# Linear attention into an MLP: the attention's small products of a batch gathered into one place of the schedule

## The chip, the core and the metric

The kernel runs on one core of a Trainium2 chip. The core has a matrix engine (TensorE, PE in the profile; PEld is its weight load), a vector engine (VectorE, DVE), a scalar engine for activations (ScalarE, ACT), a general engine (GpSimd, POOL) and a queue engine (SyncE, SP) that here only issues DMAs. Each runs its own instructions in order and waits on semaphores for the others. Matmuls write PSUM, which the kernel uses as eight banks of 512 float32 per partition. The metric is the device time of one execution in microseconds (us), less is better.

## The reference

`q`, `k` and `v` have 8 batches, 8 heads, 576 tokens and 64 values per head. The MLP takes the attention's output as 4608 tokens of 512 values.

```python
phi = lambda x: np.where(x > 0, x, np.exp(x) - 1.0) + 1.0
q_p, k_p = phi(q), phi(k)
kv  = einsum('bhsd,bhse->bhde', k_p, v)      # 64 x 64 for each head
z   = sum(k_p, axis=2)
num = einsum('bhsd,bhde->bhse', q_p, kv)
den = einsum('bhsd,bhd->bhs', q_p, z) + 1e-06
x   = (num / den) as [4608, 512]
h   = x @ w_in                               # 512 -> 2048
g   = gelu_tanh(h)
out = g @ w_out                              # 2048 -> 512
```

## The kernel before, in words

**Tiles.** Of each batch's 576 tokens the first 512 are four chunks of 128; the last 64 are its rest tokens. The rest tokens of all eight batches are 512 as well, as four tiles m = 0 to 3, each with two batches' rests. So the MLP runs in nine groups of 512 tokens, `iteration(j)` (L739): j = 0 to 7 are the batches, j = 8 is the rests. Matmul operands are bf16, sums float32.

**A group.** It has 32 slots. Slots 0 to 15 are the h steps: four matmuls of 128x512 into one PSUM bank (`h_mm`, L380) and a gelu on ACT (L390). Slots 16 to 31 are the o steps: four output tiles, each of four slots of four matmuls (`o_mm`, L723). An o tile is copied out of PSUM when its sixteen matmuls are done (`evac`, L684: DVE for t = 0 and 2, ACT for t = 1 and 3) and stored by a DMA from ACT's queue. Groups 0 and 1 interleave their steps a little differently.

**The schedule is written out by hand.** `at(j, slot, fn)` (L498) puts a piece of work behind a slot of a group; `run` calls it there, so its instructions stand at that place in each engine's order. Nothing is reordered later.

**Attention.** phi is taken as min(max(x + 1, 1), exp(x)): `linear_of` (DVE, L226), `exp_of` (ACT, L218; the exponential and the gelu use different tables, so a table load stands before and after) and `least_of` (DVE, L232). `kv` is 72 matmuls of 64x64 weights by 65 columns (the 65th column, of ones, gives z; `kv_paired`, L248). `n` holds num and den: for batches 4 to 7 `n_quads` (L278) takes for a chunk 16 matmuls of 64x64 weights by 65 columns, four at a time in the four quarters of the array, into two banks of 4 x 65 columns. `divide` (L289) makes x of it: a reciprocal of the dens (L294) and a multiply (L295) for each bank, or one of each over a pair of banks. A DMA transpose from SP's queue brings a chunk's x into `xt`, which the next group's h steps read; others bring q's phi into `qt` and a rest tile's into `qtr`.

**PSUM.** Six banks are a pool (`ps_b`) that h, o, and some n and kv tiles share; two more are one tile, the pair (`ps_a`).

**What stands where, for batch b = 4 to 7.** It is prepared two groups before its own, in group b - 2: the maps of k and q at slots 13 to 17 or 19, v's cast at 15 (20 for b = 4). In group b - 1, slot 4 (`early`): n of chunks 1 and 0 and of rest tile m = b - 4, in one run of 48 small matmuls. Slot 22 (`late`): n of chunks 3 and 2 (32), then the 72 of kv of batch b + 1, the divides, kv's copy into bf16 (L669), and the min and the transposes of q for batch b + 1 and of the next rest tile. kv of batch 4 has a place of its own in group 3, slot 2 (L617). Batches 0 to 3 go another way (`nab`, L264) that the change leaves alone.

**Loads.** SP issues all of them in order with the transposes. Seven load buffers (`pld`) are shared by q, k, v and weights. k of batch 5 is loaded at slot 11 of group 2, its q and v at slot 23; batch 6 and 7 at slot 6 of group b - 3, behind a rest tile.

Of the kernel before, what the change touches and what calls it, by code (L numbers as in the profile page):

```python
# [9 lines left out]
BF16 = mybir.dt.bfloat16  # L10
# [5 lines left out]
def kernel(  # L16
# [12 lines left out]

    nc = tc.nc

    B, H, S, D = q.shape
    d_model, d_ff = moe_w_in.shape
    P = 128
# [15 lines left out]
    pe = ctx.enter_context(tc.tile_pool(name="pe", bufs=1))  # L52
    pphi = ctx.enter_context(tc.tile_pool(name="pphi", bufs=2))
    pt = ctx.enter_context(tc.tile_pool(name="pt", bufs=2))
    px = ctx.enter_context(tc.tile_pool(name="px", bufs=5))
    pg = ctx.enter_context(tc.tile_pool(name="pg", bufs=1))
    pout = ctx.enter_context(tc.tile_pool(name="pout", bufs=2))
    psm = ctx.enter_context(tc.tile_pool(name="psm", bufs=2))
    pkv = ctx.enter_context(tc.tile_pool(name="pkv", bufs=1))
    ps_b = ctx.enter_context(  # L60
# [15 lines left out]
    def bank(name, shape, dt=FP32):  # L76
        return ps_b.tile(shape, dt, name=name, tag="b")

    def pair_of_banks(name):
        return ps_a.tile([P, 2, 512], FP32, name=name, tag="a")  # L80
# [131 lines left out]
    def exp_of(name, b, hs=None):  # L212
        x = ld[name, b]
        hs = hs or slice(0, x.shape[1])
        if (name, b) not in exps:
            exps[name, b] = pe.tile([P, x.shape[2] // D, x.shape[1], D], BF16, name=name + "_e")
        o, i = maps_view(name, b, x, exps[name, b], hs)
        nc.scalar.activation(o, i, AF.Exp)  # L218

# [8 lines left out]
    def least_of(name, b, hs=None):  # L228
        p, e = phi[name, b], exps[name, b]
        if hs:  # L230
            p, e = p[:, :, hs, :], e[:, :, hs, :]
        nc.vector.tensor_tensor(p, p, e, op=ALU.min)  # L232
# [9 lines left out]
    def kv_paired(b, ii, kv_of):  # L242
        kp, vp = phi["k", b], vp_paired(b)
        for j in range(J):
            for s in range(2):
                for a in range(2):
                    r, u = slice(HP * a, HP * (a + 1)), 2 * ii + s
                    nc.tensor.matmul(  # L248
                        kv_of(a, ii)[HP * s : HP * (s + 1)],
                        lhsT=kp[r, j, u, :],  # L250
                        rhs=vp[r, j, u, :],
                        start=(j == 0),
                        stop=(j == J - 1),
                        skip_group_check=True,
                    )
# [15 lines left out]
    def kv_of_head(b, s, i):  # L271

        r = slice(HP * s, HP * (s + 1))
        return kvs[b % 4][r, i, :] if b > 3 else kvbds[b][r, i, E * s : E * (s + 1)]

    def n_quads(qt_c, bs, ns):

        for i in range(NP):  # L278
            for t in range(2):
                for s in range(2):  # L280
                    c = slice(HP * t, HP * (t + 1))
                    nc.tensor.matmul(  # L282
                        ns[s][c, E * i : E * (i + 1)],
                        lhsT=qt_c[HP * s : HP * (s + 1), i, c],
                        rhs=kv_of_head(bs[t], s, i),
                        skip_group_check=True,
                    )

    def divide(x_v, n_v):  # L289

        heads = tuple(slice(None) for _ in n_v.shape[:-1])
        shape = list(n_v.shape[:-1])
        r = psm.tile(shape, FP32, name="r" + "".join(str(d) for d in shape[1:]))
        nc.vector.reciprocal(r, n_v[heads + (D,)])  # L294
        nc.vector.tensor_tensor(  # L295
            x_v,
            n_v[heads + (slice(0, D),)],
            r[heads + (None,)].to_broadcast(shape + [D]),
            op=ALU.mult,
        )  # L300

    def x_tile():
        return px.tile([P, d_model], BF16, name="x")
# [1 line left out]
    def by_parity(x):  # L305
        return x.rearrange("p (u a d) -> p a u d", a=2, d=D)

    def by_half(x):
        return x.rearrange("p (i s a d) -> p s a i d", s=2, a=2, d=D)

    def nab(qt_c, b):
        x, n_ps = x_tile(), pair_of_banks("n_ps")
        nab_mm(qt_c, kvbds[b], [n_ps[:, a] for a in range(2)])
# [7 lines left out]
            divide(by_parity(x)[:, a], ns[a].rearrange("p (u e) -> p u e", e=E))  # L321
        return x

    def nab_quads(qt_c, bs):

        n_ps = pair_of_banks("n_ps")
        n_quads(qt_c, bs, [n_ps[:, s] for s in range(2)])

        def x_of():
            x = x_tile()  # L330
            n_v = n_ps[:, :, 0 : NP * E].rearrange("p s (a i e) -> p s a i e", a=2, e=E)
            divide(by_half(x), n_v)
            return x

        return x_of

    def nab_quads_in_banks(qt_c, bs):
        ns = [bank("n_ps", [P, NP * E]) for _ in range(2)]
        n_quads(qt_c, bs, ns)

        def x_of():
            x = x_tile()
            for s in range(2):
                divide(by_half(x)[:, s], ns[s].rearrange("p (a i e) -> p a i e", a=2, e=E))
            return x

        return x_of

# [149 lines left out]
    def at(j, slot, fn, *args):  # L498


        fill.setdefault((j, slot), []).append((fn, args))
# [71 lines left out]
    def plan_prepare(b, s_linear, s_exp):  # L573
        def casts():
            cast_v_paired(b, slice(0, NP), nc.vector.tensor_copy)

        order = "qk" if b < 5 else "kq"

        def exps_all():
            for n in order:  # L580
                exp_of(n, b)

        j, s = s_linear
        for i, n in enumerate(order):
            at(j, s + i, linear_of, n, b)
        at(j, s + (7 if b == 4 else 2), casts)
        j, s = s_exp
        at(j, s, exps_all)
        if b < 5:
            at(j, s + 2, least_q, b)  # L590
            at(j, s + 4, least_of, "k", b)
        else:
            at(j, s + 2, least_of, "k", b)

    def transposed_q(b, cs):
        for c in cs:
            nc.sync.dma_start_transpose(
                out=qts[b][:, c],
                in_=phi["q", b][:, c].rearrange("p h d -> p (h d)"),
            )  # L600

    def least_q(b, m=None):

        least_of("q", b)
        qts[b] = pt.tile([P, C, NP, P], BF16, name="qt")
        transposed_q(b, (0, 1))
        if m is not None:
            least_rest(m)
        transposed_q(b, (2, 3))

    def kv_in_pair(b):
        kv_ps = pair_of_banks("kv_ps")
# [28 lines left out]
    def plan_attention(b):  # L641


        j, m = b - 1, b - 4

        def pair_of_chunks(c):
            in_banks = nab_quads_in_banks(qts[b][:, c + 1], (b, b))
            in_pair = nab_quads(qts[b][:, c], (b, b))
            return (c + 1, in_banks), (c, in_pair)

        def early():
            chunks = pair_of_chunks(0)
            rest = nab_quads_in_banks(rest_qt[m], (2 * m, 2 * m + 1))
            transposed_x(b, 1, chunks[0][1]())
            x = rest()
            nc.sync.dma_start_transpose(out=xt_rest[:, :, P * m : P * (m + 1)], in_=x)
            transposed_x(b, 0, chunks[1][1]())

        def late():
            chunks = pair_of_chunks(2)  # L660
            if b + 1 < B:
                kv_ps = [bank("kv_ps", [P, 2, E]) for _ in range(2)]
                for ii in range(2):
                    kv_paired(b + 1, ii, lambda a, ii: kv_ps[a][:, ii, :])
            for c, x_of in chunks:
                transposed_x(b, c, x_of())
            if b + 1 < B:
                for a in range(2):
                    nc.vector.tensor_copy(out=kvs[(b + 1) % 4][:, 2 * a : 2 * a + 2, :], in_=kv_ps[a])  # L669
                least_q(b + 1, b - 3)  # L670

        at(j, 4, early)
        at(j, 22, late)

    def least_rest(m):
        linear_of("qr", m)
        least_of("qr", m)
        rest_qt[m] = psm.tile([P, NP, P], BF16, name="qtr")
        nc.sync.dma_start_transpose(
            out=rest_qt[m], in_=phi["qr", m][:, 0].rearrange("p h d -> p (h d)")  # L680
        )

    def evac(dst, src, on_scalar):
        (nc.scalar.copy if on_scalar else nc.vector.tensor_copy)(dst, src)  # L684
# [94 lines left out]
    at(1, 10, load_all_pairs, "k", k, 4)  # L779
    plan_prepare(3, (1, 24), (1, 23))  # L780
    at(1, 23, gelu_table)
    at(1, 29, load_rest, 0)
    at(1, 29, load_q, 4)
    at(1, 29, load_all_pairs, "v", v, 4)
    at(2, 11, load_all_pairs, "k", k, 5)
    at(2, 23, load_rest, 1)
    at(2, 23, load_q, 5)
    at(2, 23, load_all_pairs, "v", v, 5)
    at(3, 2, kv_in_pair, 4)
    for b in range(4, B):  # L790
        plan_prepare(b, (b - 2, 13), (b - 2, 15))
        plan_attention(b)
        at(b - 2, 15, exp_of, "qr", b - 4)
    at(2, 22, least_rest, 0)
    for b in range(6, B):
        at(b - 3, 6, load_rest, b - 4)
        at(b - 3, 6, load_batch, b)
    for b in range(4, B):
        at(b - 2, 15, gelu_table)

    for j in range(B + 1):
        iteration(j)
# [30 lines left out]
```

## Time and profile before

| | |
|---|---|
| median of 5 runs | 284.72 us (284.67 to 284.79) |
| the profiled execution: time, span in the trace | 284.78 us, 283.0 us |
| PE busy | 274.5 us, 97% of the span |
| ACT busy | 162.0 us, 57% |
| DVE busy | 105.9 us, 37% |
| POOL busy | 15.5 us, 5%, none after 45 us |
| h matmuls L380 (incl. the rest group) | 128.3 us |
| o matmuls L723 | 126.2 us |

The span is what the trace covers; 1.78 us of the execution's time lie around it. "Busy" of PE is the union of matmul intervals whose ends are modelled, so the view to trust for small changes is the chain of waits in order of time: it names, piece by piece, what the end of the kernel waited for.

### The profile page before, as it was taken

The numbers are of one execution on the slowest core, as the hardware profiler recorded it, in microseconds if no ns is written. First come the engines' busy times: TensorE is split into PE (matmuls) and PEld (weight loads), VectorE is DVE, ScalarE is ACT, GpSimd is POOL, SyncE is SP. The second block draws the span as 40 slices with busy tenths as digits, with TensorE's granted clock in tenths as the row PEclk, the third lists the DMA queues.
The fourth block names the chain that finished last, engine by engine and source line by source line (L and its number), as shares of the span: only waits on it lengthen the run. The fifth ranks groups of instructions, "written<-read, shape, count | busy, mean of one in ns | idle before, by whom it ended". The sixth has DMA issues, their size and how long they took to land.

```text
span 283.0 us, 5373 instructions
## 1 busy us (share of the span) xinstructions
PE 274.5 (97%) x2260; PEld 135.3 (48%) x2293; DVE 105.9 (37%) x193; ACT 162.0 (57%) x222; POOL 15.5 (5%) x22
## 2 busy tenths in 40 slices
PE   8799999999999999999999999999999999999995
PEld 3474455445454445445444544454444444444444
DVE  3850386344956342727090808081403000000001
ACT  4678878786966925693468536862650265026400
POOL 4147210000000000000000000000000000000000
PEclk9999999999999999999999999999999999999999
DMA  7999999968699867997739863025301300110022
GB/s 252 400 406 397 410 402 404 404 236 224 74 232 340 231 167 220 288 367 254 157 74 331 282 170 61 0 72 160 88 19 28 126 33 0 71 80 0 0 76 74
DMA packets 59591, 53.83 MB, mean 190 GB/s; under 512 B 35760, under 2 KB 45360, under 8 KB 59568
## 3 DMA queue, kind: packets, MB, share of 16 engines
q1 hardware_dynamic: 56784, 44.58, 52.1%
q10 hardware_dynamic: 2784, 8.91, 8.4%
q8 instruction: 18, 0.29, 0.4%
q14 instruction: 5, 0.04, 0.0%
HBM read 36.70 MB, written 9.44 MB: 163 GB/s over the span
## 4 chain that ended last, share of the span: by engine, by line
PE 93%; DMA 3%; issue 1%; SPq 1%; DVE 1%; ACT 0%
PE h_ps L380 44%; PE o_ps L723 44%; DMA v_x<-in_v_dram 3%; PE kv_ps L248 2%; PE n_ps L282 1%; PE n_ps L264 1%; PE t_ps L372 1%; SPq L92 1%; SPq L97 0%; PE t_ps L526 0%; DVE vp L237 0%; DVE x L362 0%; DVE kvbd L260 0%; DVE o_sb L684 0%; PE n_ps L353 0%
## 5 line engine op out<-in xcount | busy, mean ns | idle before, releaser
L723 PE MATMUL o_ps<-w_out_sb,g 128*128 128x512 bf16 (+2 forms) x590 | 126.2, 368 | 1.4 <-issue 0.6
L380 PE MATMUL h_ps<-xt,w_in_sb 128*128 128x512 bf16 (+1 forms) x551 | 114.4, 359 | 0.8 <-issue 0.2
L390 ACT ACTIVATE g<-h_ps 128x512 bf16<-128x512 f32 x144 | 84.9, 599 | 41.3 <-PE h_ps L380 39.6
L723 PEld LDWEIGHTS <-g 128*128 128x128 bf16 x608 | 57.5, 98 | 63.9
L380 PEld LDWEIGHTS <-w_in_sb 128*128 128x128 bf16 x628 | 57.9, 98 | 62.8
L684 ACT COPY o_sb<-o_ps 128x512 f32<-128x512 f32 (+1 forms) x19 | 10.8, 575 | 64.0 <-PE o_ps L723 62.4
L684 DVE COPY o_sb<-o_ps 128x512 f32<-128x512 f32 (+1 forms) x19 | 12.2, 647 | 72.4 <-PE o_ps L723 72.4
L295 DVE TENSOR_TENSOR x<-n_ps,r 128x256 bf16<-128x256 f32 (+1 forms) x49 | 26.4, 539 | 1.7
L294 DVE RECIPROCAL r<-n_ps 128x4 f32<-128x4 f32 (+1 forms) x49 | 9.2, 187 | 36.3 <-PE n_ps L282 26.6
L232 DVE TENSOR_TENSOR k_p<-k_p,k_e 128x2304 bf16<-128x2304 bf16 (+1 forms) x9 | 11.0, 1224 | 21.1 <-ACT k_e L218 21.0
L218 ACT ACTIVATE k_e<-k_x 128x2304 bf16<-128x2304 f32 (+1 forms) x9 | 17.1, 1904 | 1.0 <-DMA k_x<-in_k_dram 1.0
L218 ACT ACTIVATE q_e<-q_x 128x2048 bf16<-128x2048 f32 (+1 forms) x9 | 15.4, 1715 | 2.8 <-DMA q_x<-in_q_dram 2.7
L226 DVE TENSOR_SCALAR q_p<-q_x 128x2048 bf16<-128x2048 f32 (+1 forms) x9 | 9.9, 1103 | 13.4 <-DMA q_x<-in_q_dram 13.4
L232 DVE TENSOR_TENSOR q_p<-q_p,q_e 128x2048 bf16<-128x2048 bf16 (+1 forms) x9 | 9.9, 1102 | 11.4 <-ACT q_e L218 11.3
L380 PE MATMUL h_ps<-xt_rest,w_in_sb 128*128 128x512 bf16 x63 | 13.9, 380 | 0.1
L226 DVE TENSOR_SCALAR k_p<-k_x 128x2304 bf16<-128x2304 f32 (+1 forms) x9 | 11.0, 1219 | 4.2 <-DMA k_x<-in_k_dram 4.2
L237 DVE CAST vp<-v_x 128x2304 bf16<-128x2304 f32 (+1 forms) x9 | 11.0, 1226 | 1.9 <-DMA v_x<-in_v_dram 1.8
L403 ACT ACT_TABLE_LOAD x8 | 10.3, 1283 | 0.1
L412 PE MATMUL w_ps<-warm 128*128 128x512 bf16 x31 | 9.0, 449 | 1.2 <-DVE warm L181 1.2
L218 ACT ACT_TABLE_LOAD x7 | 9.0, 1283 | 0.1
L141 POOL CAST w_in_sb<-w_st 128x512 bf16<-128x512 f32 (+2 forms) x6 | 7.6, 1268 | 14.2 <-DMA w_st<-in_moe_w_in_dram 14.2
L248 PE MATMUL kv_ps<-vp,k_p 64*64 64x65 bf16 x576 | 6.6, 195 | 0.9 <-DVE vp L237 0.9
(46 smaller groups left out, 74.5 us busy)
## 6 DMA issues: line engine op xcount, KB each, us to landing
out_dram<-o_sb ACTq DMA_DIRECT2D x16, 512.0 KB, 3.1
k_x<-in_k_dram SPq DMA_DIRECT2D x7, 1152.0 KB, 9.3
v_x<-in_v_dram SPq DMA_DIRECT2D x7, 1152.0 KB, 11.8
q_x<-in_q_dram SPq DMA_DIRECT2D x6, 1024.0 KB, 7.9
w_st<-in_moe_w_in_dram SPq DMA_DIRECT2D x3, 1024.0 KB, 13.4
q_x<-in_q_dram SPq DMA_DIRECT2D x4, 512.0 KB, 8.5
w_st<-in_moe_w_out_dram SPq DMA_DIRECT2D x2, 1024.0 KB, 12.6
w_st<-in_moe_w_out_dram SPq DMA_DIRECT2D x4, 512.0 KB, 11.2
```

What stands on the lines that cost most here:

```text
L218: nc.scalar.activation(o, i, AF.Exp)
L226: nc.vector.tensor_scalar(o, i, 1.0, 1.0, op0=ALU.add, op1=ALU.max)
L232: nc.vector.tensor_tensor(p, p, e, op=ALU.min)
L237: fn(out=vp_paired(b)[:, :, us, 0:D].rearrange("p j u d -> p u j d"), in_=ld["v", b][:, us].rearrange("p u (j d) -> p u j d", d=D),)
L248: nc.tensor.matmul(kv_of(a, ii)[HP * s : HP * (s + 1)], lhsT=kp[r, j, u, :], rhs=vp[r, j, u, :], start=(j == 0), stop=(j == J - 1), skip_g ...
L294: nc.vector.reciprocal(r, n_v[heads + (D,)])
L295: nc.vector.tensor_tensor(x_v, n_v[heads + (slice(0, D),)], r[heads + (None,)].to_broadcast(shape + [D]), op=ALU.mult,)
L380: nc.tensor.matmul(h_ps[:, ts], lhsT=w_in_sb[:, c, P * m : P * (m + 1)], rhs=xt[:, c, ts], start=(c == 0), stop=(c == KM - 1), skip_group_ ...
L390: nc.scalar.activation(g[:, m, :], h_ps, AF.Gelu_apprx_tanh)
L403: nc.scalar.preload_act_table_set("gelu_apprx_tanh_and_others")
L684: (nc.scalar.copy if on_scalar else nc.vector.tensor_copy)(dst, src)
L723: nc.tensor.matmul(o_ps, lhsT=g[:, m, P * t : P * (t + 1)], rhs=w_out_sb[:, m, fs], start=(m == 0), stop=(m == MM - 1),)
```

## The change

For batches 4 to 7 `early` and `late` become one place, slot 17 of group b - 1. There the n of all four chunks is taken in one run of 64 small matmuls. Their 65-column blocks fill banks six at a time: two pool banks, two more pool banks, then the pair with the last four blocks. kv of batch b + 1 follows at once, into free columns of the pair. x becomes one tile of four chunks (`xs`, one buffer); the five divides follow each other, and each chunk's transpose is issued as soon as its part is there.

The four rest tiles are no longer spread over groups 3 to 6: their loads stand in groups 4 and 6, their maps at slots 14 to 21 of groups 5 and 6, and their n, 64 small matmuls, in one run at slot 17 of group 7.

k of batch 5 to 7 is mapped in group b - 3, a group sooner; q is mapped at slots 13 to 20 of group b - 2 and v cast at slot 4 (8 for b = 5) of that group. The loads of batches 6 and 7 move from slot 6 to slot 1 and stand in the order k, q, v. The exponential of k keeps its single buffer. The pool of single x tiles has four buffers for five.

```diff
-    px = ctx.enter_context(tc.tile_pool(name="px", bufs=5))
+    px = ctx.enter_context(tc.tile_pool(name="px", bufs=4))
+    pxs = ctx.enter_context(tc.tile_pool(name="pxs", bufs=1))
...
+    prq = ctx.enter_context(tc.tile_pool(name="prq", bufs=4))
...
+    def nab_quads(qt_cs, bs, kv_b):
+        ns = [[bank("n_ps", [P, 6 * E]) for _ in range(2)] for _ in range(2)]
+        n_pair = pair_of_banks("n_ps")
+        ns.append([n_pair[:, s] for s in range(2)])
+        units = [(c, i, a) for c in range(C) for i in range(2) for a in range(2)]
+        for n, (c, i, a) in enumerate(units):
+            g = n // 6
+            for t in range(2):
+                for s in range(2):
+                    cs = slice(HP * t, HP * (t + 1))
+                    nc.tensor.matmul(
+                        ns[g][s][cs, E * (n - 6 * g) : E * (n - 6 * g + 1)],
+                        lhsT=qt_cs[c][HP * s : HP * (s + 1), 2 * a + i, cs],
+                        rhs=kv_of_head(bs[c][t], s, 2 * a + i),
+                        skip_group_check=True,
+                    )
+        if kv_b is not None:
+            for ii in range(2):
+                kv_paired(kv_b, ii, lambda a, ii: n_pair[:, a, E * (4 + ii) : E * (5 + ii)])
+        def x_of(transposed):
+            x = pxs.tile([P, C, d_model], BF16, name="xs")
+            x_v = x.rearrange("p c (i s a d) -> p s (c i) a d", s=2, a=2, d=D)
+            for g in range(2):
+                for s in range(2):
+                    divide(
+                        x_v[:, s, 3 * g : 3 * (g + 1)],
+                        ns[g][s].rearrange("p (k a e) -> p k a e", a=2, e=E),
+                    )
+                for c in ((0,), (1, 2))[g]:
+                    transposed(c, x[:, c])
+            n_v = n_pair[:, :, 0 : 4 * E].rearrange("p s (k a e) -> p s k a e", a=2, e=E)
+            divide(x_v[:, :, 6:8], n_v)
+            transposed(3, x[:, 3])
+            if kv_b is not None:
+                nc.vector.tensor_copy(
+                    out=kvs[kv_b % 4].rearrange("p (a i) e -> p a i e", a=2),
+                    in_=n_pair[:, :, 4 * E : 6 * E].rearrange("p a (i e) -> p a i e", e=E),
+                )
+        return x_of
...
+    def plan_prepare_late(b):
+        j = b - 3
+        if b == 5:
+            at(j, 15, exp_of, "k", b)
+            at(j, 22, linear_of, "k", b)
+        else:
+            at(j, 12, linear_of, "k", b)
+        at(j + 1, 8 if b == 5 else 4, cast_v_paired, b, slice(0, NP), nc.vector.tensor_copy)
+        at(j + 1, 13, linear_of, "q", b)
+        at(j + 1, 15, exp_of, "q", b)
+        if b > 5:
+            at(j, 15, exp_of, "k", b)
+        at(j + 1, 20, least_q, b)
+        at(j, 22, least_of, "k", b)
+
+    def plan_rest(m):
+        j = 5 + m // 2
...
+        at(j, 14, linear_of, "qr", m)
+        at(j, 15, exp_of, "qr", m)
+        at(j, 21, least)
...
-        at(j, 4, early)
-        at(j, 22, late)
+        def attention():
+            if b < B:
+                bs = [(b, b)] * C
+                x_of = nab_quads([qts[b][:, c] for c in range(C)], bs, b + 1 if b + 1 < B else None)
+                x_of(lambda c, x: transposed_x(b, c, x))
+            else:
+                x_of = nab_quads(rest_qt, [(2 * m, 2 * m + 1) for m in range(C)], None)
...
+        at(b - 1, 17, attention)
...
-    for b in range(4, B):
-        plan_prepare(b, (b - 2, 13), (b - 2, 15))
+    plan_prepare(4, (2, 13), (2, 15))
+    for b in range(5, B):
+        plan_prepare_late(b)
+    for m in range(C):
+        plan_rest(m)
+    for b in range(4, B + 1):
         plan_attention(b)
...
     for b in range(6, B):
-        at(b - 3, 6, load_rest, b - 4)
-        at(b - 3, 6, load_batch, b)
+        at(b - 3, 1, load_all_pairs, "k", k, b)
+        at(b - 3, 1, load_q, b)
+        at(b - 3, 1, load_all_pairs, "v", v, b)
+    for m in range(2):
+        at(4, 2, load_rest, m)
+        at(6, 1, load_rest, m + 2)
+    for j in range(2, 7):
+        at(j, 15, gelu_table)
```

More of the change, by code (lines that the diff above doesn't have):

```diff
@@ L215, in exp_of @@
         if (name, b) not in exps:
-            exps[name, b] = pe.tile([P, x.shape[2] // D, x.shape[1], D], BF16, name=name + "_e")
+            e = name + ("_e" if name != "qr" or b % 2 else "_f")
+            exps[name, b] = pe.tile([P, x.shape[2] // D, x.shape[1], D], BF16, name=e)
         o, i = maps_view(name, b, x, exps[name, b], hs)
@@ L274, in kv_of_head @@
         return kvs[b % 4][r, i, :] if b > 3 else kvbds[b][r, i, E * s : E * (s + 1)]
[L276 to L287, printed above, removed]
     def divide(x_v, n_v):
@@ L306, in by_parity @@
         return x.rearrange("p (u a d) -> p a u d", a=2, d=D)
-    def by_half(x):
-        return x.rearrange("p (i s a d) -> p s a i d", s=2, a=2, d=D)
     def nab(qt_c, b):
@@ L322, in nab_in_banks @@
         return x
[L324 to L345, printed above, removed]
+    def nab_quads(qt_cs, bs, kv_b):
[36 more added lines that the diff above has]
+                )
@@ L575, in casts @@
             cast_v_paired(b, slice(0, NP), nc.vector.tensor_copy)
-        order = "qk" if b < 5 else "kq"
         def exps_all():
-            for n in order:
+            for n in "qk":
                 exp_of(n, b)
         j, s = s_linear
-        for i, n in enumerate(order):
+        for i, n in enumerate("qk"):
             at(j, s + i, linear_of, n, b)
@@ L588, in plan_prepare, with least, least_q @@
         at(j, s, exps_all)
-        if b < 5:
-            at(j, s + 2, least_q, b)
-            at(j, s + 4, least_of, "k", b)
-        else:
-            at(j, s + 2, least_of, "k", b)
-    def transposed_q(b, cs):
-        for c in cs:
+        at(j, s + 2, least_q, b)
+        at(j, s + 4, least_of, "k", b)
+    def plan_prepare_late(b):
[3 more added lines that the diff above has]
+            at(j, 22, linear_of, "k", b)
+        else:
+            at(j, 12, linear_of, "k", b)
[8 more added lines that the diff above has]
+        j = 5 + m // 2
+        def least():
+            least_of("qr", m)
+            rest_qt[m] = prq.tile([P, NP, P], BF16, name="qtr")
+            nc.sync.dma_start_transpose(
+                out=rest_qt[m], in_=phi["qr", m][:, 0].rearrange("p h d -> p (h d)")
+            )
+        at(j, 14, linear_of, "qr", m)
+        at(j, 15, exp_of, "qr", m)
+        at(j, 21, least)
+    def least_q(b):
+        least_of("q", b)
+        qts[b] = pt.tile([P, C, NP, P], BF16, name="qt")
+        for c in range(C):
             nc.sync.dma_start_transpose(
@@ L600, in transposed_q @@
             )
[L602 to L609, printed above, removed]
     def kv_in_pair(b):
@@ L641, in plan_attention @@
     def plan_attention(b):
[L644 to L670, printed above, removed]
-        at(j, 4, early)
-        at(j, 22, late)
[L675 to L681, printed above, removed]
+        def attention():
[5 more added lines that the diff above has]
+                x_of = nab_quads(rest_qt, [(2 * m, 2 * m + 1) for m in range(C)], None)
+                x_of(
+                    lambda m, x: nc.sync.dma_start_transpose(
+                        out=xt_rest[:, :, P * m : P * (m + 1)], in_=x
+                    )
+                )
+        at(b - 1, 17, attention)
     def evac(dst, src, on_scalar):
@@ L781 @@
     at(1, 23, gelu_table)
-    at(1, 29, load_rest, 0)
     at(1, 29, load_q, 4)
@@ L785 @@
     at(2, 11, load_all_pairs, "k", k, 5)
-    at(2, 23, load_rest, 1)
     at(2, 23, load_q, 5)
@@ L789 @@
     at(3, 2, kv_in_pair, 4)
-    for b in range(4, B):
-        plan_prepare(b, (b - 2, 13), (b - 2, 15))
+    plan_prepare(4, (2, 13), (2, 15))
[4 more added lines that the diff above has]
+    for b in range(4, B + 1):
         plan_attention(b)
-        at(b - 2, 15, exp_of, "qr", b - 4)
-    at(2, 22, least_rest, 0)
     for b in range(6, B):
-        at(b - 3, 6, load_rest, b - 4)
-        at(b - 3, 6, load_batch, b)
-    for b in range(4, B):
-        at(b - 2, 15, gelu_table)
+        at(b - 3, 1, load_all_pairs, "k", k, b)
[6 more added lines that the diff above has]
+        at(j, 15, gelu_table)
     for j in range(B + 1):
```

## The prediction

> **What bounds the kernel now.** I read the page's busy times first, then the chain of waits, then the timelines of PE, DVE and SP around the moved work.
>
> ```profile
> PE 274.5 (97%) x2260; PEld 135.3 (48%) x2293; DVE 105.9 (37%) x193; ACT 162.0 (57%) x222; POOL 15.5 (5%) x22
> PEclk9999999999999999999999999999999999999999
> PE 93%; DMA 3%; issue 1%; SPq 1%; DVE 1%; ACT 0%
> ```
>
> PE is busy for 97% of the span at the full granted clock, and 93% of the chain is PE. So a change counts by the PE time that it saves or the PE waits that it makes; other engines' time counts only where it turns into such a wait. The chain in order of time shows it group by group (start, length, what):
>
> ```profile
> 136.64 3.02 PE h_ps L380 x14
> ...
> 140.95 0.54 PE n_ps L282 x48
> 141.49 0.32 PE h_ps L380
> ...
> 151.09 1.51 PE o_ps L723 x7
> ...
> 157.14 0.38 PE n_ps L282 x32
> 157.52 0.67 PE kv_ps L248 x72
> 158.19 0.16 issue
> ...
> 166.07 3.02 PE h_ps L380 x14
> ...
> 195.49 3.02 PE h_ps L380 x14
> ...
> 209.95 1.51 PE o_ps L723 x7
> ...
> 224.25 3.02 PE h_ps L380 x14
> ...
> 238.06 0.22 PE o_ps L723
> ...
> 251.88 7.99 PE h_ps L380 x37
> ```
>
> Group 7 (224.25 to 251.88) has no attention: 13.81 us for the h half, 13.82 for the o half, each 64 matmuls. That is the pace without a stall. Group 6 has n and no kv: h half 209.95 - 195.49 = 14.46, o half 14.30. Group 4: 14.45 and 14.98. So, with everything around it, the early place (48 small matmuls) costs 14.46 - 13.81 = **0.65 us**, the late one alone (32) 14.30 - 13.82 = **0.48**, and with kv 14.98 - 13.82 = 1.16, so kv behind it 0.68. No other time is lost in these groups.
>
> **PE, part by part.** The number of small matmuls does not change: 4 x (48 + 32) = 320 before, 5 x 64 = 320 after; kv follows n as it did. What changes is the number of places, eight before, five after. Now the cost of a run of 64:
>
> ```profile
> 127.64 0.45 PE L282 MATMUL n_ps<-kv,qt 64*64 64x65 bf16 x32
> 127.92 0.84 PE L248 MATMUL kv_ps<-vp,k_p 64*64 64x65 bf16 x72
> ```
>
> Start to start, 32 small matmuls take 127.92 - 127.64 = 0.28 us, 8.75 ns each; so 0.48 - 0.28 = 0.20 us of the late place is getting in and out. From there 64 cost 0.48 + 32 x 8.75 ns = 0.76; from the early place 0.65 + 16 x 8.75 ns = 0.79. The bounds: the timeline of weight loads has the first 32 of the early place in 0.26 us (111.45 to 111.71), 8.1 ns each, which gives 0.48 + 0.26 = 0.74; the straight line through the two places, (0.65 - 0.48) / 16 = 10.6 ns, gives 0.48 + 0.34 = 0.82. I take 0.77, between the two nearest rows. Before: 4 x (0.65 + 0.48) = 4.52. After: 5 x 0.77 = 3.85. **PE gains 0.67 us**, with ends 4.52 - 5 x 0.82 = 0.42 and 4.52 - 5 x 0.74 = 0.82.
>
> [...]
>
> **What the new place waits for on PE.** Four pool banks: the built order takes those of the gelus of h steps 11 to 14, each 0.60 us on ACT within its h step of 0.864; at slot 17 the latest is over 1.5 us old. The o tiles behind it take h step 15's bank and those of the first two divides, the next h steps the other two; the copy of o tile 0, now queued on DVE behind five divides, frees a bank for the third h step of the next group only. That is what is queued behind the divides, and it has some 8 us to spare.
>
> **DVE behind the new place.**
>
> ```profile
> 128.01 0.18 DVE L294 RECIPROCAL r<-n_ps 128x4 f32<-128x4 f32 x1 [0.28 <-PE n_ps L282]
> 128.22 0.42 DVE L295 TENSOR_TENSOR x<-n_ps,r 128x256 bf16<-128x256 f32 x1
> 128.56 0.17 DVE L294 RECIPROCAL r<-n_ps 128x4 f32<-128x4 f32 x1
> ...
> 129.12 0.20 DVE L294 RECIPROCAL r<-n_ps 128x8 f32<-128x8 f32 x1
> 129.35 0.69 DVE L295 TENSOR_TENSOR x<-n_ps,r 128x512 bf16<-128x512 f32 x1
> 129.96 0.48 DVE L669 CAST kv<-kv_ps 128x130 bf16<-128x130 f32 x2
> ```
>
> A divide of 256 values takes 0.55 us start to start, of 512 0.84; the new shape, 384, is not in the trace, and lies between: 0.68 to 0.70. Call t the run's start on PE. The first divide starts at t + 0.37 (127.64 to 128.01). Four take 2.75, to t + 3.1; the fifth has to wait for kv, since it reads the same tile, but kv ends at t + 0.56 + 0.67 = t + 1.2 and is hidden. It ends at t + 3.95, kv's copy and o tile 0's copy at about t + 5.1. Per group DVE does 5 divides for 8: 8 cost 6 x 0.55 + 2 x 0.84 = 4.98, 5 cost 3.6.
>
> **SP and the next group.** Chunk 0's transpose can go after the second divide, 1 and 2 after the fourth, 3 after the fifth. Undisturbed, an issue takes SP 1.2 to 1.3 us; so chunk 3's starts at about t + 5.6, and lands 3.9 us later (the median of x's transposes on the page): t + 9.5. The next h step starts at t + 0.77 + 0.68 + 14 slots of 13.82 / 16 = 0.864, some t + 13.4: **3.9 us of slack**. Before, the last x transpose of group 3 was issued at 131.2 and landed by 135.1, for an h step at 136.64: 1.5 us. The rest group has the same t + 9.5 against t + 12.8 (no kv).
>
> **Loads and maps.** In group 3, SP issues q, v of batch 5 and k, q, v of batch 6 back to back: 1024 + 1152 + 1152 + 1024 + 1152 KB = 5.6 MB, 14 us at the 400 GB/s of the busiest slices, from about 104 to 118. Their first readers are the casts and maps at slots 8, 12 and 13 (114.1 to 118.5). kv of slot 17 (122.7) needs v's cast, 1.36 us; before, v of batch 5 landed at 118.8, when it was issued later. The rests' eight loads leave the front of two load batches, 1.3 us of SP each, and stand behind those of groups 4 and 6.
>
> In group 2, ACT gets a third large exponential (k of batch 5), whose buffer must be freed by the min of batch 4's k:
>
> ```profile
> 92.57 0.52 SPq L92 DMA_DIRECT2D k_x<-in_k_dram  x1
> ```
>
> 9.3 us later (the median for k) it lands at 101.9; the exponential takes 2.1, the table 1.28, to 105.3; the copy of o tile 1 0.6, to 105.9. ACT's next work, o tile 3's copy, is due at 106.4, the first gelu at 107.4: hidden, with 0.5 us to spare there, and a late gelu costs PE nothing until six banks later. The rests' exponentials move into groups 5 and 6; group 6 gains two table loads of 1.28, hidden in ACT's 43% of idle time. The x buffers cut to four are reused a whole batch later, four transposes on: nothing.
>
> **Sum.** 0.67 us less in the profiled execution: span 283.0 to 282.3, time 284.78 to 284.11. It stands 0.06 above the median, so the median goes from 284.72 to **284.05**.
>
> **The rivals.**
> - *The time belongs to the work, not to the place* (no change). If 64 cost as 48 in proportion, 0.65 x 64 / 48 = 0.87, the new runs cost 4.33: 0.19 gained, 284.53. For it: the early place cost 0.17 more for one chunk more. Against: 8.75 ns x 16 explains 0.14 of that.
> - *The transposes take the place of the saved time* (slower). All four chunks of x now come from one place, and a late one holds the whole next group, five times over. It costs 5 us for each us beyond the slack of 3.9, so it decides from 3.9 + 0.67 / 5 = 4.0 us of lateness on; 0.5 us more gives 284.72 + 2.4 = 287.1. For it: the slowest single issues of transposes among loads took SP 2.9 us, not 1.2; three such would eat 5 us. Against: those stood amid load traffic, and no load is due between slot 17 and the group's end.
> - *The loads of group 3 land late* (slower): PE waits at kv for v's cast, once, from a landing after 122.7 + 0.5 - 1.4 = 121.8; to lose the 0.67 it takes 122.5, 3.7 us after today's landing. Against: v is issued about 2.5 us sooner.
> - *The change does not make one place of two.* The built order of PE has runs of 64 and then 72 small matmuls between two o slots, so I give it nothing.
>
> **How the numbers follow.** 0.2% of the time, 0.57 us, is about what a measurement of this kernel can tell from no change; so faster means under 284.15. The forecast, no new wait and 0.42 to 0.82 saved (283.9 to 284.3), gets 0.79; with the centre at 0.67, three quarters of it, 0.59, lie beyond 0.57 and 0.20 within. The first rival gets 0.09, all no change. The late transposes get 0.06 and the late loads 0.04, of these 0.10 together 0.08 slower and 0.02 no change. The last 0.02 go to a gain beyond 0.82. So faster 0.61, no change 0.31, slower 0.08. The range: 283.8 leaves out little below; 284.6 takes in the first rival and leaves out the late waits.
>
> **What would show it.** Right: n in runs of 64 with about 0.77 us around them; in groups 4 and 5, 27.63 + 1.45 us; an h half of 13.81 in each of groups 4 to 7; every group's first h step at PE's pace. Wrong: PE waiting at a group's first h step for a transpose of xs, at kv for a cast, or at an o tile for DVE; or a run of 64 that costs 0.9 us, which would make the forecast's step of sharing 0.20 us per place wrong.

## The result, and the profile after

The kernel after takes **284.19 us** (median of 26 runs, 284.11 to 284.53); the kernel before took 284.73 in 46 runs (284.64 to 284.99). The ratio is 0.9981, 95% interval 0.9976 to 0.9986: 0.54 us less, where 0.67 was forecast (284.05). The profiled execution took 284.38 us with a span of 282.6, against 284.78 and 283.0.

From the page of the kernel after: the busy times, the granted clock by slices, and the chain by engine.

```profile
PE 274.3 (97%) x2263; PEld 135.7 (48%) x2293; DVE 103.3 (37%) x176; ACT 164.5 (58%) x224; POOL 15.5 (5%) x22
PEclk9999999999999999999999999999999999999999
PE 93%; DMA 3%; issue 1%; SPq 1%; DVE 1%; ACT 0%
```

PE bounds the kernel as before. DVE has 17 instructions and 2.6 us less, and nothing comes of that by itself, for between 76 and 255 us no DVE work is on the chain, before or after. The chain in order of time (start, length, what) shows the new places and the beginnings of the groups (the x45 pieces; the x21 piece begins group 8):

```profile
136.46 9.71 PE h_ps L388 x45
...
152.00 0.69 PE n_ps L325 x64
152.70 0.68 PE n_ps L252 x72
...
165.57 9.71 PE h_ps L388 x45
...
194.64 9.71 PE h_ps L388 x45
...
210.18 0.69 PE n_ps L325 x64
...
223.07 9.71 PE h_ps L388 x45
...
238.61 0.69 PE n_ps L325 x64
...
251.50 4.53 PE h_ps L388 x21
```

From line to line the groups' lengths can be read: 223.07 - 194.64 = 28.43 us for group 6, and 251.50 - 223.07 = 28.43 for group 7. Group 7 without any place was 27.63, so a run of 64 costs **0.80 us**, not 0.77. Group 4 has kv too: 165.57 - 136.46 = 29.11, 0.68 more, as forecast for kv. Between 76 and 260 us PE waits for no transpose, no cast and no DVE, and the h half of each of the groups 4 to 7 takes 13.81 us, the pace without a stall.

Such lengths are the measure in what follows, taken from the first h matmul of a group to that of the next, in us:

| kernel | 3 | 4 | 5 | 6 | 7 | sum | to after |
|---|---|---|---|---|---|---|---|
| before | 30.24 | 29.43 | 29.43 | 28.76 | 27.63 | 145.48 | +0.53 |
| after | 29.92 | 29.10 | 29.08 | 28.43 | 28.43 | 144.95 | |
| e1_two_places | 30.08 | 29.27 | 29.24 | 28.59 | 28.59 | 145.78 | +0.83 |
| e2_four_places | 35.25 | 34.51 | 33.69 | 29.05 | 29.05 | 161.55 | +16.60 |
| e3_kv_apart | 30.05 | 29.24 | 29.24 | 28.43 | 28.43 | 145.38 | +0.43 |
| e4_maps_alone | 30.24 | 29.43 | 29.43 | 28.75 | 27.63 | 145.48 | +0.53 |
| e7_signals_late | 29.92 | 29.10 | 29.08 | 28.37 | 28.37 | 144.84 | -0.11 |
| e8_kv_first | 29.84 | 29.03 | 29.03 | 28.43 | 28.43 | 144.74 | -0.21 |
| e9_kv_first_signals_late | 29.79 | 28.97 | 28.97 | 28.37 | 28.37 | 144.48 | -0.47 |
| e11_four_places_sooner | 30.48 | 29.67 | 29.64 | 29.05 | 29.05 | 147.89 | +2.94 |

The sums differ by 0.53 us between before and after, the medians by 0.54: the whole change lies in these five groups. Outside them the profiled executions scatter: group 2 begins between 76.8 and 77.5 us, whichever kernel it is. The lengths do not: e5_one_transpose repeats those of after, and e4_maps_alone those of before, to 0.01 us. That is why the lengths tell apart what one execution's time can't.

### The profile page after: what moved, and what is told of

Same layout as the page of the kernel before. It is cut to its first block, busy times and chain, and to the rows that moved or that the text cites. A ratio compares the mean times of both kernels' runs of the same rounds, so it can differ in the third digit from the quotient of the medians.

```text
span 282.6 us, 5347 instructions
## 1 busy us (share of the span) xinstructions
PE 274.3 (97%) x2263; PEld 135.7 (48%) x2293; DVE 103.3 (37%) x176; ACT 164.5 (58%) x224; POOL 15.5 (5%) x22
## 4 chain that ended last, share of the span: by engine, by line
PE 93%; DMA 3%; issue 1%; SPq 1%; DVE 1%; ACT 0%
PE h_ps L388 44%; PE o_ps L725 44%; DMA v_x<-in_v_dram 3%; PE n_ps L325 1%; PE kv_ps L252 1%; PE n_ps L268 1%; PE n_ps L252 1%; PE t_ps L380 1%; SPq L95 1%; SPq L100 0%; PE t_ps L534 0%; DVE vp L241 0%; DVE x L370 0%; DVE kvbd L264 0%; DVE o_sb L686 0%
## 5 line engine op out<-in xcount | busy, mean ns | idle before, releaser
L285 DVE RECIPROCAL r<-n_ps 128x6 f32<-128x6 f32 (+2 forms) x42 | 8.1, 193 | 58.8 <-PE n_ps L325 49.1
L286 DVE TENSOR_TENSOR xs<-n_ps,r 128x384 bf16<-128x384 f32 (+1 forms) x25 | 14.6, 584 | 0.9
L286 DVE TENSOR_TENSOR x<-n_ps,r 128x512 bf16<-128x512 f32 (+1 forms) x17 | 10.7, 629 | 0.6
```

The costliest lines, as they stand in the source:

```text
L286: nc.vector.tensor_tensor(x_v, n_v[heads + (slice(0, D),)], r[heads + (None,)].to_broadcast(shape + [D]), op=ALU.mult,)
```

## The experiments

The ratios are to the kernel before, run on the same chip.

### Is it the number of places?

**e1_two_places** takes n in two runs of 32, at slots 17 and 18, kv behind the second; the divides as after.

```diff
-        for n, (c, i, a) in enumerate(units):
+        def part(ns_):
+            for n in ns_:
+                c, i, a = units[n]
...
+            state["a"][0](range(0, 16 // 2))
...
-        at(b - 1, 17, attention)
+        at(b - 1, 17, begin)
+        at(b - 1, 18, more, 1)
+        at(b - 1, 18, end)
```

> The changed kernel with its run of 64 small matmuls cut into 32 at slot 17 and 32 (with kv behind them) at slot 18, in all five groups; the divides follow the second part. Theory (each place costs about 0.18 us on PE, whatever stands in it; the small matmuls 9.6 ns each): five places more, +0.89 us on the changed kernel's 284.19, 285.08, +0.12% on the kernel before, with about 0.49 us around 32 and 1.16 around 32 and kv. Rival 1 (the cost goes with the matmuls): no change, 284.19. [...]

Measured: 285.18 us, ratio 1.0013 (1.0003 to 1.0022); the gain is gone. The groups sum to 0.83 us more than after, for five places more.

**e3_kv_apart** leaves n in one run of 64 and puts kv at a place of its own, slot 18.

```diff
-        at(b - 1, 17, attention)
+        at(b - 1, 17, begin)
+        at(b - 1, 18, end)
```

> The changed kernel with the 64 small matmuls of n at slot 17 and kv a place of its own at slot 18 (three groups; the divides follow it). Theory (a place costs the same whatever stands in it): three places more, +0.54 us, 284.73, no change against the kernel before. Rival (kv costs the same alone as behind n): 284.19.

Measured: 284.86 us, ratio 0.9995 (0.9986 to 1.0005). Groups 3 to 5, which alone have a kv, are 0.13 to 0.16 longer than after; groups 6 and 7 are as after. So the place costs, and it does not matter whether n or kv stands there. But 0.13 to 0.16 us a place is less than the 0.20 of the forecast; the next section but one says why.

**e2_four_places** takes n in four runs of 16 at slots 17 to 20.

```diff
-        at(b - 1, 17, attention)
+        at(b - 1, 17, begin)
+        at(b - 1, 18, more, 1)
+        at(b - 1, 19, more, 2)
+        at(b - 1, 20, more, 3)
+        at(b - 1, 20, end)
```

> The same cut into four places of 16, at slots 17, 18, 19 and 20, kv behind the last. Theory: fifteen places more, +2.7 us, 286.9, +0.75% on the kernel before; a place of 16 costs about 0.33 us. Rival 1: no change. [...] If the divides' later start (2.6 us) ate the slack of the x transposes, PE would wait at a group's first h step, and the time would be beyond 287.

Measured: 301.3 us, ratio 1.058 (1.0546 to 1.0614), far more than 15 places more can explain at 0.2 us. The view of waits of e2 has one large line (what waited for what: us in total, times, longest us):

```profile
PE h_ps L393 <- DMA xt<-xs: 9.2, 3, 4.6
```

SP's timeline of e2 in group 3 (start, length, engine, line, what, instructions):

```profile
127.10 6.18 SPq L637 DMA_TRANSPOSE qt<-q_p  x4
133.39 5.14 SPq L660 DMA_TRANSPOSE xt<-xs  x4
```

PE's timeline of e2 at the start of group 4 (in brackets the idle time before, and its releaser):

```profile
141.42 2.72 PE L393 MATMUL h_ps<-xt,w_in_sb 128*128 128x512 bf16 x6 [4.61 <-DMA xt<-xs]
```

The granted clock in e2, by 40 slices of the span:

```profile
PEclk9999999999999999998799989999999999999999
```

The step that forms q's minimum and issues q's four transposes also stands at slot 20, and there it comes ahead of the divides. So SP issued q's transposes first (127.10), which nobody needs for a whole group, and x's only from 133.39. PE, done with the o steps, stood idle for 4.61 us until 141.42, and 9.2 us in three groups. With the first two waits (4.61 us until 141.42, and 2.36 us until 175.93) the granted clock fell: it was 0.50 from 139.31 to 146.14 us and from 176.86 to 180.27, and 1.00 between and behind; the third wait, 2.20 us until 209.62, had no such stretch with it. PE was busy for 4.50 and 3.19 us of the two stretches. Six h matmuls took 2.72 us from 141.42, at 0.50, and 1.46 us from 209.62, at 1.00; if the work of the two stretches takes about half as long at 1.00, an estimate of 3.8 us comes on top of the 9.2. Together they are 13.0 of the 161.55 - 147.89 = 13.66 us by which e2's five groups are longer than those of the next kernel. Groups 6 and 7, where q has no transposes, are 29.05 and show no wait. This is the second rival of the prediction, seen at work; that it needs only the wrong order on SP is what the next kernel tests.

**e11_four_places_sooner** tests that reading. The four places move to slots 16 to 19, so that the divides and x's transposes come ahead of q's step.

```diff
-        at(b - 1, 17, begin)
-        at(b - 1, 18, more, 1)
-        at(b - 1, 19, more, 2)
-        at(b - 1, 20, more, 3)
-        at(b - 1, 20, end)
+        at(b - 1, 16, begin)
+        at(b - 1, 17, more, 1)
+        at(b - 1, 18, more, 2)
+        at(b - 1, 19, more, 3)
+        at(b - 1, 19, end)
```

> The kernel e2_four_places again (four places in a group for n, each with its kv behind it or alone), but with the four places moved ahead of the step that forms q's minimum and its transposes, and the divides, x and its transposes straight behind the last of them. Theory (a place costs about 0.2 us and no more; the other 14 us of e2 came from its order on SyncE, where q's transposes stood ahead of x's): no wait of TensorE at the first h of a group, and by the group lengths of e2's last two groups, which had no q transposes (29.05 us against 28.43 after, 0.6 us more each), five groups give about 2.8 us over after, 287.0 us, ratio about 1.008. Rival (four places stall x's transposes by themselves, since the divides come later in the group): over 290 us, with waits of 2 us and more at the first h of groups 4 to 6.

Measured: 287.29 us, ratio 1.0083 (1.0066 to 1.01). SP's timeline of e11 in group 3:

```profile
128.15 5.58 SPq L660 DMA_TRANSPOSE xt<-xs  x4
133.82 6.46 SPq L637 DMA_TRANSPOSE qt<-q_p  x4
```

Its granted clock by slices:

```profile
PEclk9999999999999999999999999999999999999999
```

With x first, PE waits for no transpose, the clock stays, and 301.3 - 287.29 = 14.0 us are back: they were never the price of the places. (x's transposes begin 133.39 - 128.15 = 5.24 us sooner. The places also stand one slot sooner, but a slot is only 0.86 us.) What is left is 2.94 us by the groups for 15 places more. Groups 6 and 7 say it most cleanly, three places more and 29.05 - 28.43 = 0.62, 0.21 us each. So the theory holds, and the rival, that four places stall the transposes by themselves, falls.

### Is it the maps, the loads or the order of the transposes?

**e4_maps_alone** is the kernel before with the new places of the loads and of the maps of k, q and v, and with n, and the rest tokens, where they were.

```diff
+        if b == 5:
+            at(j, 15, exp_of, "k", b)
+            at(j, 22, linear_of, "k", b)
+        else:
+            at(j, 12, linear_of, "k", b)
...
+        at(b - 3, 1, load_all_pairs, "k", k, b)
+        at(b - 3, 1, load_q, b)
+        at(b - 3, 1, load_all_pairs, "v", v, b)
         at(b - 3, 6, load_rest, b - 4)
-        at(b - 3, 6, load_batch, b)
```

> The kernel before with one part of the change alone: k of batches 5 to 7 mapped a group sooner, q's maps and v's casts and the loads of batches 6 and 7 placed as in the changed kernel; the two places of n and the spread rest tiles stay. Theory (the moved maps and loads cost PE nothing): 284.73, ratio 1.000, within 0.1%. Rival (the sooner loads or the exponential of k that waits for the single buffer cost something that the merged runs pay back): slower by 0.1 to 0.5 us, and then PE waits at a kv or at a gelu's bank in groups 2 or 3.

Measured: 284.99 us, ratio 1.0007 (0.9998 to 1.0016), and the groups as before, but for 0.01 us. By the groups the maps and loads neither give nor take; they only make the new place possible.

**e5_one_transpose** is after with q's four transposes in one instruction.

```diff
-        for c in range(C):
-            nc.sync.dma_start_transpose(
-                out=qts[b][:, c],
-                in_=phi["q", b][:, c].rearrange("p h d -> p (h d)"),
-            )
+        nc.sync.dma_start_transpose(
+            out=qts[b].rearrange("p c i n -> p (c i) n"),
+            in_=phi["q", b].rearrange("p c h d -> p (c h d)"),
+        )
```

> The changed kernel with the four transposes of a batch's q put into one DMA transpose of 128x2048, so that the run of 64 waits for one semaphore of q's and not for four. Theory A (the run costs 0.80 and not 0.77 us because PE's weight loads stop some 26 ns at waits inside the run): the two gaps of 34 ns among the weight loads of each run go or get fewer, 0.03 to 0.08 us less in each of four groups, 0.1 to 0.3 us in all, 283.9 to 284.1. Theory B (small matmuls cost 9.6 ns, stops or none): no change in PE, 284.19. If the one transpose takes much longer than four, nothing waits for it for 25 us.

Measured: 284.24 us, ratio 0.9981 (0.9971 to 0.999), group by group as after. SP spent 3.11 us on the issue in group 3 instead of 5.49. So neither that time of SP nor the waits of the run on several transposes are what makes it 0.80.

### Where the 0.03 us of a run come from

Among the starts of the weight loads of a run, most follow each other by 3 to 26 ns, by 8 on average. A few are 33 to 35 ns behind the load before them. This table, worked from the trace, gives for groups 3 to 7 the places of these gaps (the load behind the gap, counted from 0):

| kernel | groups | run | gap ahead of load |
|---|---|---|---|
| before | 3 to 6 | early 48 | 47 |
| before | 3 to 5 | late 32 + 72 of kv | 47, 48, 64 |
| before | 6 | late 32 | none |
| after | 3, 4 | 64 + 72 of kv | 55, 56, 79, 80, 96 |
| after | 5 | 64 + 72 of kv | 55, 56, 79, 80 |
| after | 6, 7 | 64 | 55, 56 |
| e1_two_places | 3 to 7 | first 32 | none |
| e1_two_places | 3, 4 | second 32 + 72 of kv | 47, 48, 64 |
| e1_two_places | 5 | second 32 + 72 of kv | 47, 48 |
| e1_two_places | 6, 7 | second 32 | none |
| e3_kv_apart | 3 to 7 | 64 | 55, 56 |
| e3_kv_apart | 3 to 5 | 72 of kv | none |
| e7_signals_late | 3, 4 | 64 + 72 of kv | 71, 72, 79, 80, 96 |
| e7_signals_late | 5 | 64 + 72 of kv | 71, 72, 79, 80 |
| e7_signals_late | 6, 7 | 64 | none |
| e8_kv_first | 3 to 5 | 72 of kv + 64 | 127, 128 |
| e8_kv_first | 6, 7 | 64 | 55, 56 |
| e9_kv_first_signals_late | 3 to 5 | 72 of kv + 64 | none |
| e9_kv_first_signals_late | 6, 7 | 64 | none |

The matmuls of a run that signal another engine (raise a semaphore that it waits for) explain them; the trace tells which they are. In the run of 64 as it is built, counted from 0, these are numbers 22, 23, 46, 47 and 63, each the last into a bank. In group 5 the 63rd signals nothing, and kv's last does it. 33 loads on from them are 55, 56, 79, 80 and 96: exactly the gaps, as far as the run reaches. In the early 48 (14, 15, 46, 47), only 14 + 33 = 47 still falls inside, and 15 + 33 = 48 is just outside; the late 32 alone (14, 15, 31) ends before any. **A signal shows on PE only where at least 33 more small matmuls follow it in the same run**; otherwise nothing of it shows in the groups' lengths. Each gap costs about 34 - 8 = 26 ns. Before there are 3 x (1 + 3) + 1 = 13 of them, after 5 + 5 + 4 + 2 + 2 = 18: 5 x 26 ns = 0.13 us, as much as the result lacks of the 0.67. If that is right, the gaps can be moved at will; three kernels do so.

**e7_signals_late** takes the blocks in an order that closes the first two banks sixteen matmuls later.

```diff
-        for n, (c, i, a) in enumerate(units):
+        for n in (0, 1, 2, 3, 6, 7, 8, 9, 4, 5, 10, 11, 12, 13, 14, 15):
+            c, i, a = units[n]
```

> The changed kernel with the blocks of n taken in the order 0-3, 6-9, 4, 5, 10-15, so that the four pool banks are complete, and signal, at matmuls 38, 39, 46 and 47 of a run and not at 22, 23, 46 and 47. Theory (each signalling small matmul stops PE's weight loads for some 26 ns 33 loads later, if that still lies in the run): no gap of 34 ns in the runs of 64 of groups 6 and 7, 0.05 us less in each, 28.38 us a group and not 28.43; in groups 3 and 4 the gaps move from loads 55 and 56 to 71 and 72 and their number stays five; 284.09 in all. Rival (the gaps come from the length of the run, as its head start runs out): they stay at 55 and 56, 284.19.

Measured: 284.17 us, ratio 0.9974 (0.9964 to 0.9984). The signals stand at 38, 39, 46, 47 and 63 now. In the runs with kv the first two gaps move by 16 loads, as the signals do, and these groups' lengths stay to 0.01 us. In the runs of 64 no gap is left, and groups 6 and 7 are 28.43 - 28.37 = 0.06 us shorter, two gaps each, with the same five signals. e7 also settles another reading, that a gap comes from the change to other banks: its order changes banks behind matmuls 15 and 31 too, where nothing signals, and no gap stands 33 loads on, at 48 or 64.

**e8_kv_first** puts the 72 of kv ahead of the 64 of n.

```diff
+        if kv_b is not None:
+            for ii in range(2):
+                kv_paired(kv_b, ii, lambda a, ii: n_pair[:, a, E * (4 + ii) : E * (5 + ii)])
         for n, (c, i, a) in enumerate(units):
...
-        if kv_b is not None:
-            for ii in range(2):
-                kv_paired(kv_b, ii, lambda a, ii: n_pair[:, a, E * (4 + ii) : E * (5 + ii)])
```

> The changed kernel with kv's 72 small matmuls ahead of the 64 of n in the same place (groups 3 to 5). Theory: of the five signals of n only the first two lie 33 loads before the run's end, so five gaps become two in groups 3 and 4 and four become two in group 5: 0.08, 0.08 and 0.05 us less, 283.98. Rival (length of the run): no change, 284.19. The divides start 0.6 us later, within the slack of the transposes.

Measured: 284.26 us, ratio 0.9973 (0.9963 to 0.9982). n's first signals stand at 72 + 22 and 72 + 23 of 136 now; 33 on are 127 and 128, the only gaps left. Groups 3 and 4, which lose three gaps, are 0.08 and 0.07 shorter, group 5, which loses two, 0.05.

**e9_kv_first_signals_late** does both.

> Both: kv first, and the order of blocks with late signals. Theory: no gap of 34 ns in any run; 0.13, 0.13, 0.10, 0.05 and 0.05 us less in groups 3 to 7, 0.47 us, 283.72, ratio to before 0.9964. Rival (length of the run): no change, 284.19, ratio 0.9981.

Measured: 283.89 us, ratio 0.9967 (0.9954 to 0.9979). No gap is left in any run. Groups 3 to 7 are shorter than after by 0.13, 0.13, 0.11, 0.06 and 0.06 us, for 5, 5, 4, 2 and 2 gaps: 26 ns each, as near as 0.01 us can tell. It is the lengths that show this; the ratios of e7, e8 and e9 have intervals that overlap that of after (0.9976 to 0.9986). The timeline of the weight loads shows it in one line for the run of group 6 (start, length, engine, line); this is after's:

```profile
210.11 0.65 PEld L325 LDWEIGHTS <-qt 64*64 64x64 bf16 x64 [0.42 <-issue]
```

And this is e9's:

```profile
209.55 0.60 PEld L329 LDWEIGHTS <-qt 64*64 64x64 bf16 x64 [0.42 <-issue]
```

The same 64 loads take 0.65 and 0.60 us. The two gaps of 26 ns are this difference.

The gap explains e1 and e3 as well. A place of e3's kv costs 0.13 (group 3) or 0.16 (group 5) net, but with it three or two gaps go, 0.08 or 0.05 us; so the place itself costs 0.21. In e1's groups 6 and 7 it is 0.16 + 2 x 0.026 = 0.21 too. And the trace says it directly: from the last 128x512 matmul to the first small one 93 ns pass beyond its 216, and from the last small one to the next 128x512 one, where the trace has its record, 120 to 127 ns, where the usual pitch is 8: 0.21 us. So the whole change adds up: three places fewer at 0.21 to 0.22 us are 0.63 to 0.66, less 0.13 for five gaps more 0.50 to 0.53, and the groups show 0.53.

### Can it be carried further?

**e6_batch3** takes batch 3 by the new place too, in group 2 at slot 17, and so removes four places of four matmuls of 128x128 weights; kv of batches 3 and 4 keep their places.

```diff
-                x_of = nab_quads([qts[b][:, c] for c in range(C)], bs, b + 1 if b + 1 < B else None)
+                x_of = nab_quads([qts[b][:, c] for c in range(C)], bs, b + 1 if 3 < b < B - 1 else None)
...
-    plan_by_chunks(3, 2, 2, 4)
+    at(2, 2, kv_in_pair, 3)
+    plan_attention(3)
```

> The changed kernel, and batch 3 too is taken in one run of 64 small matmuls at slot 17 of group 2, in place of four times four full-size matmuls of 128x130; its kv stays where it is. Full-size ones cost PE 4 x 0.236 = 0.94 us in the trace of before, with nothing for getting in, a run of 64 without kv 0.80. Theory: 0.14 us less, 284.05, ratio to before 0.9976. Rival (x of batch 3 now comes late, behind batch 4's maps on DVE): PE waits at the first h step of group 3, up to 1 us, 284.2 to 285.

Measured: 284.18 us, ratio 0.9976 (0.9967 to 0.9985); group 2 is 29.24 for 29.37, the others are as after. A gain of 0.13 us, which the time alone would not have shown.

**e10_with_batch3** is e9 and e6 together.

> The same, and batch 3 in one run of 64 too. Theory: 0.14 us for batch 3 and 0.05 for the two gaps of its run on top, 283.53, ratio to before 0.9958. Rival: as batch 3 alone had it, 284.05, 0.9976.

Measured: **283.77 us, ratio 0.9961 (0.9948 to 0.9973)**; in the same comparison before took 285.02. It beats both kernels: its interval ends below that of after (0.9976). Its chain in group 2 shows batch 3's n as one place:

```profile
91.96 1.89 PE o_ps L726 x8
93.85 0.64 PE n_ps L329 x61
94.49 0.16 issue
```

The piece is 0.64 us long, as in the chain of e9's group 6, where after's is 0.69. Group 2 is 29.19 us, groups 3 to 7 are those of e9.

## Why the prediction was right, and where a size was off

**PE per place: right.** The forecast had 0.20 us for getting in and out, and eight places made five. Measured 0.21 (e1, e3, the starts in the trace; e11's groups 6 and 7 give 0.21, or 0.22 with the two gaps that go there). The first rival, that the time belongs to the work, would have made e1 as fast as after and falls with it: five places more cost 0.83 us and no matmul was added.

**The run of 64: the mis-sized term.** Forecast 0.77 (0.74 to 0.82), measured 0.80, so 5 x 0.03 = 0.15 us of the 0.67 are missing, to the 0.13 to 0.14 that the sums show. The mechanism, sharing the way in and out, was right; this size was not. The forecast drew a line through rows whose signals were mostly hidden: the late 32 had no gap, the early 48 one. The run of 64 has two, because merging brings signals far enough from the run's end to be seen. Without them (e9, groups 6 and 7) it costs 28.37 - 27.63 = 0.74, the forecast's lower end, which goes by the pitch of 32 loads without a gap.

**The signals.** Of n's matmuls in these groups 28 signal in the trace before and 24 after. Counted alike, at the 26 ns measured here, that would be a gain, by estimate 4 x 26 ns = 0.10 us; but those that show rise from 13 to 18, the loss of 0.13 us above. So where the signals stand in a run counted for more here than how many there are.

**DVE: right.** The timeline of DVE after, in group 3, where the run starts at t = 122.83 (start, length, engine, line, and the idle time before):

```profile
123.27 0.20 DVE L285 RECIPROCAL r<-n_ps 128x6 f32<-128x6 f32 x1 [1.72 <-PE n_ps L325]
123.50 0.56 DVE L286 TENSOR_TENSOR xs<-n_ps,r 128x384 bf16<-128x384 f32 x1
123.97 0.18 DVE L285 RECIPROCAL r<-n_ps 128x6 f32<-128x6 f32 x1
...
126.29 0.69 DVE L286 TENSOR_TENSOR xs<-n_ps,r 128x512 bf16<-128x512 f32 x1
126.89 0.42 DVE L350 CAST kv<-n_ps 128x260 bf16<-128x260 f32 x1
127.23 0.68 DVE L686 COPY o_sb<-o_ps 128x512 f32<-128x512 f32 x1
```

A divide of 384 takes 0.70 from start to start (123.27 to 123.97; forecast 0.68 to 0.70). The fifth ends at 126.98, t + 4.15 (forecast t + 3.95), kv's copy and o tile 0's copy at t + 5.1, as forecast. The banks come free in time: no o tile waits.

**The next group's x: right, with more room.** SP after, in group 3:

```profile
107.91 7.88 SPq L95 DMA_DIRECT2D v_x<-in_v_dram  x1
124.81 5.20 SPq L655 DMA_TRANSPOSE xt<-xs  x4
130.10 5.49 SPq L632 DMA_TRANSPOSE qt<-q_p  x4
```

The four transposes of x are issued by 130.01, t + 7.2, about what t + 5.6 and 1.3 us for the last gave (t + 6.9). The last begins at 128.79 and lands 2.3 us later, at 131.11, not 3.9 later as forecast; the next h step begins at 136.30, so the room is 5.2 us, where 3.9 was forecast. (The forecast's own terms, 0.77 + 0.68 + 14 x 0.864, give t + 13.5 for that h step, not t + 13.4; it came at t + 13.47.) The rival that the transposes come late did not come to pass, and e2 shows what it would have cost, and e11 that the order on SP decides it.

**Loads and maps: right that they cost nothing, with other landings than forecast.** e4 shows the first. v of batch 5 was to land before 121.8; its cast began at 116.24, after 5.9 us of waiting on DVE, 5.6 us in time. k of batch 6 came late enough that its map waited 1.44 us on DVE, with nothing behind it that PE needed. The third exponential of group 2 ended with its table at 103.45 (forecast 105.3), and ACT then waited 2.5 us for its next o tile, where 0.5 had been left to spare. That the loads' issues back to back would hold SP until 115.8 (the first line above) was not forecast; it delayed nothing, for SP had no transpose due before 124.8.

**The numbers.** 284.19 lies in the range (283.8 to 284.6), and 0.04 us above the bound of 284.15 that parted faster from no change; by the ratio the gain is 0.19% (0.14 to 0.24). The forecast had put three quarters of its chance beyond the bound on a centre of 0.67, and it is the 0.03 us by which each run of 64 was forecast too cheap that put the result on its edge.

## What to carry to other kernels

In a kernel that PE bounds at 97%, moving between long 128x512 matmuls and packed 64x64 ones costs here a fixed 0.21 to 0.22 us in every place, for 16, 32, 64 or 72 small matmuls alike, so such places are worth merging, and the work that makes it possible (maps and loads a group sooner) can be free. When runs are merged, look where their signals stand: one that has 33 or more small matmuls behind it cost 26 ns here, one nearer to the end of the run nothing that the lengths show, so matmuls that close a bank belong late, and what needs no early signal goes first. And where one place feeds the whole next group, its transposes must come first on their queue: in e2 the wrong order of eight issues in each of three groups cost 14 us, waits and lower clock together.

## What was not expected of the hardware

- A signal's cost on PE falls 33 small matmuls later, and vanishes if the run has ended by then (all 28 runs of n in batches 4 to 7 and the rests of before, after, e7, e8 and e9, without exception). Where the 33 come from was not tested.
- SP's issue of one load of 1152 KB took 7.88 us (107.91, shown above) in group 3, as the last of five loads of 5504 KB together; the first three took 0.53, 0.53 and 0.66, the fourth 2.26. What limits it was not tried; the view of SP's waits puts 7.9 us down to a gelu of ACT, so it may be a wait and not the issue itself.
- One transpose of four chunks' q took SP 3.11 us in e5, where four took 5.49 in after.
- Waits of PE of 4.61 and 2.36 us in e2 went with a granted clock of 0.50 for 6.83 and 3.41 us, and a wait of 2.20 us with none. In after, where PE waits in these groups for nothing but 0.2 us of issue at a time, every slice shows 0.9 or more. Where between 2.20 and 2.36 us the difference lies, or whether it lies in the length at all, was not tried.
